# Attention, leaky-ReLU MLP and gated MLP on one core: results of the last layer turned in 32x32 blocks on VectorE and stored in runs of 64 features

## Chip, cores, metric

The kernel runs on one core of a Trainium2 chip. The metric is device time in microseconds (us), the median of several runs; smaller is better.

## What is computed

The reference, cut to its core (all in float32):

```python
# q, k, v: (8, 8, 576, 64); attention inside chunks of 64 positions
attn = softmax(q_c @ k_c.T / 8)              # per chunk
x = (attn @ v).transpose(0, 2, 1, 3).reshape(4608, 512)
h = x @ w_in                                  # 512 -> 2048
x = (max(h, 0) + alpha * min(h, 0)) @ w_out   # 2048 -> 512
g, val = x @ w_gate, x @ w_val                # 512 -> 1536 each
out = (silu(g) * val) @ w_out2                # 1536 -> 512, out is (4608, 512)
```

## The kernel before

**Layout.** Activations stand with features on the 128 partitions and tokens along the row. The 4608 tokens are nine blocks of 512 (`NB`); blocks 0 to 7 are the first 512 positions of each of the eight sequences, block 8 holds the last 64 of each. Every float32 product is three passes in `fp32r` (`mm3`, lines 522 to 524): an operand is split into a high part (a copy, ACT or VectorE) and a low part (a subtraction, VectorE), by `split`.

**Products of block pairs.** Two blocks are worked as a 2x2 block product with seven products in place of eight (numbers `p` 5, 1, 6, 2, 7, 3, 4 in `layer2`, `ORDER2`; 1 to 4 of operands `g`, 5 to 7 of sums). Each sums up in PSUM banks: X0, X1 for p 1, 6, 7, 4, one upon the other; W0, W1 for 5 and 3; Y0, Y1 for 2. So a bank X must be read between two of these products. Quarter `c` of the result (0 to 3: half `c // 2` of the 512 features, block `c % 2` of the pair), each in two tiles `m` of 128 features, is finished after p = 2 (c 0), 7 (c 3), 3 (c 1) and 4 (c 2).

**The last layer and its output.** `mlp_b` runs the gated MLP for the pairs (1, 2), (3, 4), (5, 8), (6, 7); its second layer hands each finished PSUM tile to `to_out` (line 762). There VectorE adds PSUM and a saved part into one of eight spare tiles (for c 2 a copy does), tokens along the row. Once a block has its four tiles, TensorE transposes them against `ident` into bank a0 or a1, four 128x128 pieces for each 128 tokens (line 781); a copy takes the bank to one of three tiles `c`, and `store_rows` (line 759) stores 128 tokens with 2 KB rows. Block 0 is computed the other way round, tokens on the partitions (`plain2(..., natural=True)`, line 661), and stored from `c` as it is. The weights of the last layer are split by `out2_quad` through `make` in the middle of the kernel, stored in `l_out2`, and read back by each pair.

**Order of the work.** All steps go into a `Program` with an engine, a guessed cost and their dependences. `order()` gives each step a due time from the main products that depend on it (a step on which no product depends has none and comes last) and lays the engines' streams in order of time. All DMAs are issued from SP, in that order; a DMA whose data are not there holds those behind it.

Of the kernel before, what the change touches and what calls it, by code (L numbers as in the profile page):

```python
# [13 lines left out]
ALU = mybir.AluOpType  # L14
# [3 lines left out]
P = 128  # L18
# [107 lines left out]
def act(n):  # L126
    return 0.17 + n * 0.84e-3


def dve2(n):  # L130
    return 0.15 + n * 1.05e-3
# [5 lines left out]
def dve1(n):  # L137
    return 0.1 + n * 0.53e-3
# [3 lines left out]
def attention_moe_moe2(ctx, tc, q, k, v, w_in, w_out, alpha, w_gate, w_val, w_out2, out):  # L142
# [24 lines left out]
    B, H, S, D = q.shape  # L167
# [3 lines left out]
    CH = 64  # L171
    KD = DM // P
    HP = H // 2
    NB = 512
    NCH = NB // CH
    NBLK = NT // NB
    JA = FF // (2 * P)
    JB = FF2 // (2 * P)
    scale = 1.0 / float(D) ** 0.5
    G = 256  # L180

    pr = Program()
    nv, na, ng, npe, nsp = nc.vector, nc.scalar, nc.gpsimd, nc.tensor, nc.sync
# [6 lines left out]
    def one(name, shape, dtype=F32):  # L190
        return sb.tile(shape, dtype, name=name, tag=name)

    KF = FF // P
    ident = one("ident", [P, P])
# [1 line left out]
    nalpha_sb = one("nalpha_sb", [P, KF])  # L196
    zero = one("zero", [P, KF])
    ops = Ring(sb, "op", 14, [P, 2, NB], F32R)
    gts = [[one(f"g{j}_{c}", [P, NB]) for c in range(4)] for j in range(JA)]
    xin = Ring(sb, "xin", 4, [P, NB], F32)  # L200
    sring = Ring(sb, "s", 6, [P, NB], F32)
    hring = Ring(sb, "h", 2, [P, NB], F32)
# [4 lines left out]
    cs = Ring(sb, "c", 3, [P, NB], F32)  # L207
# [8 lines left out]
    bank = {b: ps.tile([P, NB], F32, name=b, tag=b) for b in ("X0", "X1", "W0", "W1", "Y0", "Y1", "a0", "a1")}  # L216
# [4 lines left out]
    def item(engine, cost, fn, reads=(), writes=(), port=False, **kw):  # L221
        pr.add([(engine, cost, fn, port)], reads, writes, **kw)

    def dma(nbytes, fn, reads=(), writes=(), lat=2.2, **kw):
        item("SP", 0.06 + nbytes / 390e3, fn, reads, writes, lat=lat, **kw)


    def copy_(dst, src, n, reads, writes, psum=True, **kw):
        pr.add([("ACT", act(n), lambda: na.activation(out=dst, in_=src, func=AF.Copy), False),  # L229
                ("DVE", dvep(n) if psum else dve1(n), lambda: nv.tensor_copy(dst, src), not psum)],  # L230
               reads, writes, **kw)

    def add2(dst, a, b, op, n, reads, writes, psum=False, **kw):
        item("DVE", dve2(n), lambda: nv.tensor_tensor(out=dst, in0=a, in1=b, op=op), reads, writes, **kw)  # L234

    def split(hi, lo, src, n, rkeys, hkey, lkey, **kw):
        copy_(hi, src, n, rkeys, [hkey], psum=False, **kw)
        add2(lo, src, hi.bitcast(F32), ALU.subtract, n, [*rkeys, hkey], [lkey], **kw)
# [51 lines left out]
    lay_out2 = Layer("l_out2", [(j, p) for p in [*ORDER2, 21] for j in range(JB)])  # L290
# [4 lines left out]
    def rows(w, m):  # L295
        return w[m * P:(m + 1) * P, :]

    def convert(src, into=None, after=None):

        raw, rk = raws.next()  # L300
        rk = [rk, rk + (0,), rk + (1,)]
        c, ck = into or cs.next()
        dst = raw.rearrange("p a b -> p (a b)")
        if len(src.shape) == 3:
            dst = dst.rearrange("p (a f) -> p a f", a=src.shape[1])
        dma(NB * 8 * P, lambda: nsp.dma_start(out=dst, in_=src), [], rk, after=after)

        lw, lk = tring.next()  # L310
        lw, cu = lw.bitcast(U32), c.bitcast(U32)
        item("ACT", 0.66, lambda: na.activation(out=c, in_=raw[:, :, 1].bitcast(F32), func=AF.Abs, scale=2.0 ** -112),
             rk, [ck])
        item("DVE", 0.4, lambda: nv.tensor_scalar(out=lw, in0=raw[:, :, 0], scalar1=29, scalar2=None,
                                                   op0=ALU.logical_shift_right), rk, [lk], port=True)
        item("DVE", 0.69, lambda: nv.scalar_tensor_tensor(out=cu, in0=cu, scalar=3, in1=lw, op0=ALU.logical_shift_left,
                                                          op1=ALU.bitwise_or), [lk], [ck], port=True)
        item("DVE", 0.69, lambda: nv.scalar_tensor_tensor(out=cu, in0=raw[:, :, 1], scalar=0x80000000, in1=cu,
                                                         op0=ALU.bitwise_and, op1=ALU.bitwise_or),
             rk, [ck], port=True)  # L320
        return c, ck

    LO, HI = slice(0, G), slice(G, 2 * G)

    def sums(c0, k0, c1, k1, by_cols):

        if by_cols:
            a11, a12, a21, a22 = (c0[:, LO], k0), (c0[:, HI], k0), (c1[:, LO], k1), (c1[:, HI], k1)
        else:
            a11, a12, a21, a22 = (c0[:, LO], k0), (c1[:, LO], k1), (c0[:, HI], k0), (c1[:, HI], k1)  # L330
        ta, ka = tring.next()
        tb, kb = tring.next()
        s1, s2, s3, s4 = (ta[:, LO], ka), (ta[:, HI], ka), (tb[:, LO], kb), (tb[:, HI], kb)

        def comb(d, a, b, op):
            add2(d[0], a[0], b[0], op, G, [a[1], b[1]], [d[1]])

        comb(s1, a21, a22, ALU.add)
        comb(s2, s1, a11, ALU.subtract)
        comb(s3, a11, a21, ALU.subtract)  # L340
        comb(s4, a12, s2, ALU.subtract)
        return {1: a11, 2: a12, 3: s4, 4: a22, 5: s1, 6: s2, 7: s3, 21: a21}
# [10 lines left out]
                self.t, self.k = self.ring.next()  # L353
            return self.t[:, self.h], self.k + (self.h,)

    def make(layer, use, src, dst):

        t, key = dst
        split(t[:, 0], t[:, 1], src[0], G, [src[1]], key, key)
        layer.put(use, t, key)  # L360
        return t, key

# [358 lines left out]
    def silu(x, c, acc, b, s, n):  # L721
# [11 lines left out]
        else:  # L733
            add2(g, src, g, ALU.mult, n, rd, [gk, *wr], psum=s is None)


    spare = [(gts[j][c], ("g", j, c)) for j in range(JB, JB + 2) for c in range(4)]
    flip = [0]

    def row_runs(s0, n):  # L740

        runs, t = [], s0
        while t < s0 + n:
            i, r = divmod(t, NB)
            if i < B:
                m = min(s0 + n - t, NB - r)
                row = i * S + r
            else:
                c, r = divmod(r, CH)
                m = min(s0 + n - t, CH - r)  # L750
                row = c * S + NB + r
            runs.append((t - s0, m, row))
            t += m
        return runs

    def store_rows(e, ek, s0, w):
        def store():
            for a, k_, row in row_runs(s0, w):
                nsp.dma_start(out=out[row:row + k_, :], in_=e[a:a + k_])
        dma(w * NB * 4, store, [ek], [])  # L760

    def to_out(m, c, acc, b, s, n, pair, got):
        t, tk = spare[(2 * (c >= 2) + m) + 4 * (c % 2)]
        h = t[:, :n]
        if s is not None:
            add2(h, acc, s[0], ALU.add, n, [s[1]], [tk, b], psum=True)
        else:
            copy_(h, acc, n, [], [tk, b])
        col = c % 2
        got.setdefault(col, set()).add((c, m))  # L770
        if len(got[col]) < 4:
            return
        src = [spare[f + 4 * col] for f in range(KD)]
        for o0 in range(0, n, P):
            w = min(P, n - o0)
            bk = f"a{flip[0] % 2}"
            flip[0] += 1

            def tr(o0=o0, w=w, bk=bk):
                for f in range(KD):  # L780
                    npe.transpose(bank[bk][:w, f * P:(f + 1) * P], src[f][0][:, o0:o0 + w], ident)  # L781
            item("PE", 0.45, tr, [x[1] for x in src], [bk])
            e, ek = cs.next()
            copy_(e[:w], bank[bk][:w], NB, [], [ek, bk])

            store_rows(e, ek, pair[col] * NB + o0, w)

    def gkey(j, c):
        return gts[j][c], ("g", j, c)
# [32 lines left out]
    chalves = Halves(cring)  # L822
# [24 lines left out]
    def out2_quad(j, after):  # L847
        c = [z for m in (2 * j, 2 * j + 1) for z in convert(rows(w_out2, m), after=pr.mains[after])]
        bl = sums(*c, False)
        for p in (1, 21, 2, 4, 5, 6, 7, 3):  # L850
            make(lay_out2, (j, p), bl[p], chalves.next())

    with tc.manual_schedule():
        make_identity(nc, ident)
# [40 lines left out]
        def mlp_b(pair, weights, between=lambda: None):  # L895
            o = operands(x2d, "x2", pair, xin8)
            layer1(qb, NB, o, weights, act_b)
            between()
            layer2(JB, NB, lay_out2, partial(to_out, n=NB, pair=pair, got={}))
# [27 lines left out]
        x = load_x(x1d, "x1", 8)  # L927
# [4 lines left out]
        for j in range(4):  # L932
            out2_quad(j, m0 + 6 * j)
        m0 = len(pr.mains)
        mlp_a((4, 5), got_in)
        for j in range(4, JB):
            out2_quad(j, m0 + 20 * (j - 4))
# [4 lines left out]
        half = cring.t[0].bitcast(F32).rearrange("p h a g -> p h (a g)")  # L942
# [14 lines left out]
        plain2(JB, [(0, XW)], partial(stored, lay_out2, OUT, lambda j: j), natural=True)  # L957
        for a, b in enumerate(XW):
            e, ek = cs.next()
            copy_(e, bank[b], NB, [], [ek, b])  # L960
            store_rows(e, ek, a * P, P)

        assert sring.i % sring.n == 0
        mlp_b((1, 2), second_quads(lay_b, lambda x: [*keep[x][0], *keep[x][1]]))
# [8 lines left out]
        warm, t, seq = True, 0.0, pr.order()  # L973
        for s, _, engine, cost, fn, main in seq:
            if engine == "PE" and warm:
# [5 lines left out]
                t = s + cost  # L981
# [33 lines left out]
```

## Time and profile before

| | |
|---|---|
| runs | 1749.92, 1748.27, 1744.92 us; median 1748.27 |
| profiled execution | 1743.0 us, span of its instructions 1741.2 us |
| granted TensorE clock, mean | 0.989 of full |
| busy share of the span | TensorE 95%, its weight loads 78%, VectorE 70%, ScalarE 54% |
| DMA | 407.58 MB in 321588 packets; 73.3% of 16 engines' span |

A view's row gives what it says for one execution: busy time, how often, the mean of one, and what ended the idle time before. PE is TensorE, DVE is VectorE, ACT ScalarE; SPq rows are DMA issues of SP. A timeline row merges equal instructions that follow each other (x8) into start, length and form.

### The profile page before, as it was taken

The numbers are of one execution on the slowest core, as the hardware profiler recorded it, in microseconds if no ns is written. First come the engines' busy times: TensorE is split into PE (matmuls) and PEld (weight loads), VectorE is DVE, ScalarE is ACT, GpSimd is POOL, SyncE is SP. The second block draws the span as 40 slices with busy tenths as digits, with TensorE's granted clock in tenths as the row PEclk, the third lists the DMA queues.
The fourth block names the chain that finished last, engine by engine and source line by source line (L and its number), as shares of the span: only waits on it lengthen the run. The fifth ranks groups of instructions, "written<-read, shape, count | busy, mean of one in ns | idle before, by whom it ended". The sixth has DMA issues, their size and how long they took to land.

```text
span 1741.2 us, 26558 instructions
## 1 busy us (share of the span) xinstructions
PE 1661.1 (95%) x9388; PEld 1352.7 (78%) x9388; DVE 1215.6 (70%) x2156; ACT 935.7 (54%) x1649; POOL 1.0 (0%) x8
## 2 busy tenths in 40 slices
PE   6898998999889799999999999999999999999998
PEld 5777886778767577877888788778878888788886
DVE  5787886898666689777666954588769544864482
ACT  5677545774353677554444544464675533643362
POOL 0000000000000000000000000000000000000000
PEclk9999999999999899999999999999999999999999
DMA  8978878778999895888755577886765855555563
GB/s 197 261 246 242 283 260 266 239 215 237 248 264 308 315 354 190 274 269 291 267 196 188 191 217 235 221 248 217 235 211 190 285 195 193 189 199 193 193 209 129
DMA packets 321588, 407.58 MB, mean 234 GB/s; under 512 B 175280, under 2 KB 195760, under 8 KB 321456
## 3 DMA queue, kind: packets, MB, share of 16 engines
q1 hardware_dynamic: 319392, 405.89, 73.3%
q8 instruction: 74, 1.21, 0.3%
q14 instruction: 58, 0.48, 0.1%
q10 hardware_dynamic: 2064, 0.01, 0.1%
HBM read 307.24 MB, written 98.57 MB: 233 GB/s over the span
## 4 chain that ended last, share of the span: by engine, by line
PE 52%; DMA 2%; DVE 2%; ACT 1%; issue 0%; ACTq 0%; SPq 0%; DVEq 0%
PE X L522 9%; PE X L523 9%; PE X L524 9%; PE W L522 5%; PE W L524 5%; PE W L523 5%; PE Y L523 2%; PE Y L522 2%; PE Y L524 2%; DMA raw<-in_moe_w_gate_dram 1%; PE X L661 1%; PE W L661 1%; DMA raw<-in_moe_w_val_dram 1%; PE a L781 1%; PE a L465 0%
## 5 line engine op out<-in xcount | busy, mean ns | idle before, releaser
L522 PE MATMUL X<-op,w 128*128 128x512 f32 x1024 | 407.8, 398 | 19.1 <-DVE h L234 12.7
L523 PE MATMUL X<-op,w 128*128 128x512 f32 x1024 | 400.8, 391 | 0.0
L524 PE MATMUL X<-op,w 128*128 128x512 f32 x1024 | 400.6, 391 | 0.0
L229 ACT ACTIVATE op<-g 128x512 fp32r<-128x512 f32 x348 | 210.8, 629 | 146.1 <-PE X L523 43.9
L234 DVE TENSOR_TENSOR op<-g,op 128x512 fp32r<-128x512 f32 x348 | 227.3, 686 | 36.6 <-ACT op L229 31.2
L522 PEld LDWEIGHTS X<-op,w 128*128 128x128 f32 x1024 | 193.2, 189 | 70.6 <-DVE h L234 17.3
L522 PE MATMUL Y<-op,w 128*128 128x512 f32 x560 | 225.0, 402 | 4.1 <-ACT g L732 2.5
L524 PEld LDWEIGHTS X<-op,w 128*128 128x128 f32 x1024 | 193.4, 189 | 41.1
L522 PE MATMUL W<-op,w 128*128 128x512 f32 x544 | 214.0, 393 | 10.6 <-ACT h L229 10.6
L523 PEld LDWEIGHTS X<-op,w 128*128 128x128 f32 x1024 | 193.5, 189 | 37.8
L523 PE MATMUL Y<-op,w 128*128 128x512 f32 x560 | 220.1, 393 | 1.8 <-DVE w L234 1.8
L524 PE MATMUL Y<-op,w 128*128 128x512 f32 x560 | 219.9, 393 | 0.0
L524 PE MATMUL W<-op,w 128*128 128x512 f32 x544 | 212.4, 390 | 0.0
L523 PE MATMUL W<-op,w 128*128 128x512 f32 x544 | 212.2, 390 | 0.0
L229 ACT ACTIVATE s<-X 128x512 f32<-128x512 f32 x172 | 102.3, 596 | 107.5 <-PE X L524 106.2
L234 DVE TENSOR_TENSOR h<-Y,s 128x512 f32<-128x512 f32 x78 | 53.7, 689 | 137.7 <-PE Y L524 136.5
L522 PEld LDWEIGHTS Y<-op,w 128*128 128x128 f32 x560 | 106.5, 190 | 28.3 <-ACT g L732 2.9
L522 PEld LDWEIGHTS W<-op,w 128*128 128x128 f32 x544 | 102.4, 188 | 33.2 <-ACT h L229 11.4
L703 DVE SCALAR_TENSOR_TENSOR g<-h,nalpha_sb,g 128x512 f32<-128x512 f32 x143 | 106.7, 746 | 28.9 <-ACT h L695 28.6
L523 PEld LDWEIGHTS Y<-op,w 128*128 128x128 f32 x560 | 106.6, 190 | 23.8 <-DVE w L234 2.8
L524 PEld LDWEIGHTS Y<-op,w 128*128 128x128 f32 x560 | 106.1, 190 | 22.8
L524 PEld LDWEIGHTS W<-op,w 128*128 128x128 f32 x544 | 102.4, 188 | 21.6
(136 smaller groups left out, 2070.0 us busy)
## 6 DMA issues: line engine op xcount, KB each, us to landing
w<-l_out SPq DMA_DIRECT2D x168, 512.0 KB, 3.8
w<-l_b SPq DMA_DIRECT2D x126, 512.0 KB, 4.2
w<-l_in SPq DMA_DIRECT2D x56, 512.0 KB, 4.5
l_b<-w SPq DMA_DIRECT2D x84, 256.0 KB, 3.3
l_out<-cw SPq DMA_DIRECT2D x80, 256.0 KB, 5.0
l_in<-w SPq DMA_DIRECT2D x64, 256.0 KB, 4.0
raw<-in_moe_w_out_dram SPq DMA_DIRECT2D x28, 512.0 KB, 5.2
w<-l_in SPq DMA_DIRECT2D x56, 256.0 KB, 4.9
```

Of the source, the lines that this page charges most:

```text
L229: pr.add([("ACT", act(n), lambda: na.activation(out=dst, in_=src, func=AF.Copy), False), ("DVE", dvep(n) if psum else dve1(n), lambda: nv. ...
L234: item("DVE", dve2(n), lambda: nv.tensor_tensor(out=dst, in0=a, in1=b, op=op), reads, writes, **kw)
L522: npe.matmul(out=acc, lhsT=w[:, 0, wk], rhs=x[:, 0, :n], start=first, stop=False, skip_group_check=True)
L523: npe.matmul(out=acc, lhsT=w[:, 1, wk], rhs=x[:, 0, :n], start=False, stop=False, skip_group_check=True)
L524: npe.matmul(out=acc, lhsT=w[:, 0, wk], rhs=x[:, 1, :n], start=False, stop=stop, skip_group_check=True)
L661: npe.matmul(out=acc, lhsT=t[:, gp, a * P:(a + 1) * P], rhs=w[:, :, wp, :], start=first and i == 0, stop=stop and i == 2, skip_group_check ...
L703: nv.scalar_tensor_tensor(out=g, in0=h, scalar=nal, in1=g, op0=ALU.mult, op1=ALU.add)
L781: npe.transpose(bank[bk][:w, f * P:(f + 1) * P], src[f][0][:, o0:o0 + w], ident)
```

## The change

In `to_out` VectorE adds into one of the two tiles `h` (`hring`), then turns that tile in 32x32 blocks (`nv.transpose`) into a tile `turned`; for c 2 it turns straight from PSUM. A 32x32 turn leaves the tokens of a block of 32 on the partitions of their feature group, so a quarter is stored by four DMAs of 32 partitions, each with runs of 64 features (256 bytes); for block 8 by eight. For 64 consecutive features to meet, the columns of the last layer's weights are reordered when they are split (`make(..., turn=True)`), and for block 0 put back when its PSUM banks are copied, in halves of 256. The spare tiles of two `j` become four tiles `turned` of twice the width in the same place. TensorE's transposes, the copies from a0 and a1, and `store_rows` are gone.

```diff
-    gts = [[one(f"g{j}_{c}", [P, NB]) for c in range(4)] for j in range(JA)]
+    gts = [[one(f"g{j}_{c}", [P, NB]) for c in range(4)] for j in range(JB)]
+    turned = [one(f"turned{i}", [P, 2 * NB]) for i in range(2 * (JA - JB))]
+    gts += [[t[:, h * NB:(h + 1) * NB] for t in turned[2 * i:2 * i + 2] for h in range(2)] for i in range(JA - JB)]
...
+    def swapped(t, a, b):
+        return t.rearrange("p (a b i) -> p b a i", a=a, b=b)
...
-        split(t[:, 0], t[:, 1], src[0], G, [src[1]], key, key)
+        if turn:
+            split(swapped(t[:, 0], 2, 4), swapped(t[:, 1], 2, 4), src[0].rearrange("p (g m i) -> p g m i", g=4, m=2),
+                  G, [src[1]], key, key)
...
     def to_out(m, c, acc, b, s, n, pair, got):
-        t, tk = spare[(2 * (c >= 2) + m) + 4 * (c % 2)]
-        h = t[:, :n]
-        if s is not None:
-            add2(h, acc, s[0], ALU.add, n, [s[1]], [tk, b], psum=True)
-        else:
-            copy_(h, acc, n, [], [tk, b])
...
-            item("PE", 0.45, tr, [x[1] for x in src], [bk])
-            e, ek = cs.next()
-            copy_(e[:w], bank[bk][:w], NB, [], [ek, bk])
-            store_rows(e, ek, pair[col] * NB + o0, w)
+        col, half = c % 2, c // 2
+        k = 2 * col + half
+        e = turned[k].rearrange("p (t m i) -> p t m i", m=2, i=32)
+        if s is not None:
+            t, tk = hring.next()
+            h = t[:, :n]
+            add2(h, acc, s[0], ALU.add, n, [s[1]], [tk, b], psum=True)
+            rd, wr = [tk], []
+        else:
+            h, rd, wr = acc, [], [b]
+        item("DVE", 0.7, lambda: nv.transpose(out=e[:, :, m, :], in_=h.rearrange("p (t i) -> p t i", i=32)),
+             rd, [*ek, *wr])
...
+            for g in range(4):
+                gs, fs = slice(32 * g, 32 * g + 32), slice(2 * P * half + 64 * g, 2 * P * half + 64 * g + 64)
+                src = turned[k].rearrange("p (t f) -> p t f", f=64)[gs]
+                if i < B:
+                    nsp.dma_start(out=out[i * S:i * S + NB, fs].rearrange("(t p) f -> p t f", p=32), in_=src)
...
-            copy_(e, bank[b], NB, [], [ek, b])
-            store_rows(e, ek, a * P, P)
+            for h in (LO, HI):
+                copy_(e[:, h].rearrange("p (g m i) -> p g m i", g=4, m=2), swapped(bank[b][:, h], 2, 4), G, [],
+                      [ek, b])
```

**Where the order moves.** Line numbers below are those of each kernel's own file. TensorE's stream loses its 128 transposes and is otherwise the same, row for row. It ended, after the last product into X, with ten groups of four transposes; the last of these:

```order
L781 MATMUL a_163<-ident,g_0_105 128x128
L781 MATMUL a_163<-ident,g_1_106 128x128
L781 MATMUL a_163<-ident,g_2_107 128x128
L781 MATMUL a_163<-ident,g_3_108 128x128
L781 MATMUL a_164<-ident,g_0_105 128x128
L781 MATMUL a_164<-ident,g_1_106 128x128
L781 MATMUL a_164<-ident,g_2_107 128x128
L781 MATMUL a_164<-ident,g_3_108 128x128
```

Now the last product is TensorE's end, and VectorE's stream ends with the adds, the turns into `turned` (`h` are the two tiles of `hring`, X and W the banks of the product):

```order
L237 TENSOR_TENSOR h_119<-W_155,s_117 128x512
L237 TENSOR_TENSOR h_120<-W_156,s_118 128x512
L761 STREAM_TRANSPOSE turned_107<-h_119 128x16x32
L761 STREAM_TRANSPOSE turned_107<-h_120 128x16x32
L761 STREAM_TRANSPOSE turned_106<-X_153 128x16x32
L761 STREAM_TRANSPOSE turned_106<-X_154 128x16x32
```

Behind the last main product stand only two turns (from X) on VectorE, and SP's last four DMAs (of `turned_106`).

The other place is VectorE at the switch from the second layer of pair (1, 2) to the first layer of pair (3, 4), where it splits the next pair's operands (`op`, from `xin` and `raw`) between the last adds. Before:

```order
L234 TENSOR_TENSOR op_67<-raw_139,op_67 128x512
L234 TENSOR_TENSOR raw_139<-raw_139,xin_113 128x512
L234 TENSOR_TENSOR op_68<-raw_140,op_68 128x512
L234 TENSOR_TENSOR raw_140<-raw_140,xin_115 128x512
L234 TENSOR_TENSOR op_69<-xin_114,op_69 128x512
L234 TENSOR_TENSOR op_70<-xin_116,op_70 128x512
L234 TENSOR_TENSOR op_71<-raw_139,op_71 128x512
L234 TENSOR_TENSOR op_72<-raw_140,op_72 128x512
```

and now:

```order
L237 TENSOR_TENSOR op_67<-raw_135,op_67 128x512
L761 STREAM_TRANSPOSE turned_107<-h_119 128x16x32
L237 TENSOR_TENSOR op_68<-raw_136,op_68 128x512
L237 TENSOR_TENSOR raw_135<-raw_135,xin_109 128x512
L237 TENSOR_TENSOR op_69<-xin_110,op_69 128x512
L237 TENSOR_TENSOR raw_136<-raw_136,xin_111 128x512
L237 TENSOR_TENSOR op_70<-xin_112,op_70 128x512
L761 STREAM_TRANSPOSE turned_107<-h_120 128x16x32
L237 TENSOR_TENSOR op_71<-raw_135,op_71 128x512
L761 STREAM_TRANSPOSE turned_106<-X_153 128x16x32
L761 STREAM_TRANSPOSE turned_106<-X_154 128x16x32
L237 TENSOR_TENSOR op_72<-raw_136,op_72 128x512
```

Eight turns came in at this switch; the two that free X0 and X1 (ACT copies before) now stand behind the split of `op_71`.

On SP the quarter's four DMAs stand where the quarter is finished. Its stream ended with ten stores of 128 tokens; now it ends so (`w` are the weights read ahead):

```order
L262 DMA w_126<-l_out_167 128x1024
L773 DMA out_dram<-turned_105 32x16x64 x4
L262 DMA w_127<-l_out_167 128x1024
L773 DMA out_dram<-turned_108 32x16x64 x4
L773 DMA out_dram<-turned_107 32x16x64 x4
L773 DMA out_dram<-turned_106 32x16x64 x4
```

The first quarter's four DMAs moved ahead of the last weight load, and one quarter in place of ten row groups is left for the end.

## Rows read from the trace of the kernel before

**Rows 1.** Busy time by window: stretch, PE, PEld, DVE, ACT, POOL, clock, DMA share, GB/s.

```profile
500.00:600.00 100.00, 84.92 (x517) 67.50 (x516) 66.87 (x135) 45.60 (x92) 0.00 (x0) 0.91 0.93 296
1000.00:1100.00 100.00, 100.00 (x543) 82.42 (x543) 48.72 (x78) 43.71 (x71) 0.00 (x0) 1.00 0.76 226
1100.00:1200.00 100.00, 98.07 (x769) 78.20 (x768) 79.14 (x147) 55.84 (x89) 0.00 (x0) 1.00 0.84 233
1200.00:1300.00 100.00, 97.63 (x473) 80.27 (x472) 69.99 (x107) 67.24 (x116) 0.00 (x0) 1.00 0.66 223
1600.00:1700.00 100.00, 100.00 (x450) 82.79 (x449) 60.23 (x93) 47.20 (x82) 0.00 (x0) 1.00 0.58 200
```

**Rows 2.** Groups of instructions by line and form: busy us, mean ns.

```profile
L781 PE MATMUL a<-ident,g 128*128 128x128 f32 x128 | 17.8, 276 | 2.1 <-ACT c L229 2.0
L229 ACT ACTIVATE c<-a 128x512 f32<-128x512 f32 x32 | 18.3, 598 | 28.7 <-PE a L781 27.2 <-DMA out_dram<-c 0.8 <-PE W L523 0.2
L982 DVE STREAM_TRANSPOSE qT<-qk 128x512 f32<-128x512 f32 x20 | 14.1, 705 | 7.0 <-DMA qk<-in_q_dram 6.9
...
L234 DVE TENSOR_TENSOR g<-g,g 128x512 f32<-128x512 f32 x144 | 95.4, 685 | 0.9
L234 DVE TENSOR_TENSOR h<-X,s 128x512 f32<-128x512 f32 x78 | 53.6, 689 | 19.3 <-ACT g L732 8.7 <-PE X L524 5.3 <-DMA x2d<-h 2.3
L229 ACT ACTIVATE qT<-X 128x512 f32<-128x512 f32 x16 | 17.6, 1102 | 9.8 <-PE X L419 9.5 <-PE W L434 0.3
L229 ACT ACTIVATE cw<-c 128x256 fp32r<-128x256 f32 x24 | 9.7, 413 | 14.4 <-DMA l_out<-cw 13.5 <-DVE c L318 0.6 <-DVE h L234 0.3
```

**Rows 3.** Timeline of PE in the switch after pair (3, 4).

```profile
1281.67 0.39 PE L524 MATMUL X<-op,w 128*128 128x512 f32 x1
1281.90 1.04 PE L781 MATMUL a<-ident,g 128*128 128x128 f32 x8
1282.69 0.47 PE L522 MATMUL Y<-op,w 128*128 128x512 f32 x1
1283.01 0.39 PE L523 MATMUL Y<-op,w 128*128 128x512 f32 x1
1283.23 0.40 PE L524 MATMUL Y<-op,w 128*128 128x512 f32 x1
```

**Rows 4.** Timeline of PE, ACT and SP at the end.

```profile
1727.63 0.39 PE L524 MATMUL X<-op,w 128*128 128x512 f32 x1
...
1728.31 0.40 PE L524 MATMUL X<-op,w 128*128 128x512 f32 x1
1728.55 1.03 PE L781 MATMUL a<-ident,g 128*128 128x128 f32 x8
...
1737.53 0.60 ACT L229 ACTIVATE c<-a 128x512 f32<-128x512 f32 x1 [0.76 <-DMA out_dram<-c]
...
1729.81 8.67 SPq L759 DMA_DIRECT2D out_dram<-c  x10
```

**Rows 5.** Instructions on `out_dram` in the last 16 us.

```profile
L759 SPq DMA_DIRECT2D out_dram<-c x10: 332/332/338, 1729.8 to 1738.1; - x10
...
DMA to landing us min/median/max: 2.0/2.0/2.3
```

**Rows 6.** Timeline of DVE: two turns in a row.

```profile
1185.23 0.70 DVE L982 STREAM_TRANSPOSE qT<-qk 128x512 f32<-128x512 f32 x1
1185.86 0.67 DVE L982 STREAM_TRANSPOSE kT<-qk 128x512 f32<-128x512 f32 x1
```

**Rows 7.** Loads of `qk` (SP issue ns) and `v` (issue, landing), 1100 to 1200 us.

```profile
L397 SPq DMA_DIRECT2D qk<-in_q_dram x20: 332/487/1642, 1107.1 to 1177.5; - x20
...
L409 SPq DMA_DIRECT2D v<-in_v_dram x10: 601/618/1310, 1114.3 to 1173.8; - x10
DMA to landing us min/median/max: 3.0/5.3/7.7
```

**Rows 8.** Timelines at the first switch: ACT, DVE, PE.

```profile
1019.96 1.28 ACT L229 ACTIVATE g<-X 128x512 f32<-128x512 f32 x2 [0.23 <-PE X L524]
...
1019.77 0.69 DVE L234 TENSOR_TENSOR op<-raw,op 128x512 fp32r<-128x512 f32 x1 [0.66 <-ACT op L229]
...
1021.80 0.39 PE L522 MATMUL X<-op,w 128*128 128x512 f32 x1
```

**Rows 9.** Waits of PE, 1200 to 1300 and 1300 to 1400 us: us, times, longest.

```profile
PE X L522 <- DVE h L234: 1.7, 1, 1.7
...
PE X L522 <- DVE h L234: 1.5, 1, 1.5
```

**Rows 10.** The page's DMA queue (packets, MB, share) and a weight load's landing (us).

```profile
q1 hardware_dynamic: 319392, 405.89, 73.3%
...
w<-l_b SPq DMA_DIRECT2D x126, 512.0 KB, 4.2
```

More of the change, by code (lines that the diff above doesn't have):

```diff
@@ L354, in next, with make @@
             return self.t[:, self.h], self.k + (self.h,)
-    def make(layer, use, src, dst):
+    def swapped(t, a, b):
+        return t.rearrange("p (a b i) -> p b a i", a=a, b=b)
+    def make(layer, use, src, dst, turn=False):
         t, key = dst
-        split(t[:, 0], t[:, 1], src[0], G, [src[1]], key, key)
+        if turn:
+            split(swapped(t[:, 0], 2, 4), swapped(t[:, 1], 2, 4), src[0].rearrange("p (g m i) -> p g m i", g=4, m=2),
+                  G, [src[1]], key, key)
+        else:
+            split(t[:, 0], t[:, 1], src[0], G, [src[1]], key, key)
         layer.put(use, t, key)
@@ L734, in silu @@
             add2(g, src, g, ALU.mult, n, rd, [gk, *wr], psum=s is None)
[L737 to L747, printed above, removed]
-            else:
[L749 to L754, printed above, removed]
@@ L756, in store_rows, with to_out @@
-    def store_rows(e, ek, s0, w):
-        def store():
[L758 to L762, printed above, removed]
-        t, tk = spare[(2 * (c >= 2) + m) + 4 * (c % 2)]
-        h = t[:, :n]
-        if s is not None:
-            add2(h, acc, s[0], ALU.add, n, [s[1]], [tk, b], psum=True)
-        else:
-            copy_(h, acc, n, [], [tk, b])
[L769 to L781, printed above, removed]
-            item("PE", 0.45, tr, [x[1] for x in src], [bk])
-            e, ek = cs.next()
-            copy_(e[:w], bank[bk][:w], NB, [], [ek, bk])
-            store_rows(e, ek, pair[col] * NB + o0, w)
+    def to_out(m, c, acc, b, s, n, pair, got):
+        col, half = c % 2, c // 2
+        k = 2 * col + half
+        e = turned[k].rearrange("p (t m i) -> p t m i", m=2, i=32)
+        ek = [("g", JB + k // 2, 2 * (k % 2) + x) for x in range(2)]
+        if s is not None:
[3 more added lines that the diff above has]
+            rd, wr = [tk], []
+        else:
+            h, rd, wr = acc, [], [b]
+        item("DVE", 0.7, lambda: nv.transpose(out=e[:, :, m, :], in_=h.rearrange("p (t i) -> p t i", i=32)),
+             rd, [*ek, *wr])
+        got[c] = got.get(c, 0) + 1
+        if got[c] < 2:
+            return
+        i = pair[col]
+        def store():
+            for g in range(4):
[3 more added lines that the diff above has]
+                    nsp.dma_start(out=out[i * S:i * S + NB, fs].rearrange("(t p) f -> p t f", p=32), in_=src)
+                else:
+                    o3 = out.rearrange("(b s) f -> b s f", b=B)
+                    for a in range(2):
+                        nsp.dma_start(out=o3[:, NB + 32 * a:NB + 32 * a + 32, fs].rearrange("b p f -> p b f"),
+                                      in_=src[:, a::2, :])
+        dma(2 * P * NB * 4, store, ek, [])
@@ L850, in out2_quad @@
         for p in (1, 21, 2, 4, 5, 6, 7, 3):
-            make(lay_out2, (j, p), bl[p], chalves.next())
+            make(lay_out2, (j, p), bl[p], chalves.next(), turn=True)
     with tc.manual_schedule():
@@ L959, in attention_moe_moe2 @@
             e, ek = cs.next()
-            copy_(e, bank[b], NB, [], [ek, b])
-            store_rows(e, ek, a * P, P)
+            for h in (LO, HI):
+                copy_(e[:, h].rearrange("p (g m i) -> p g m i", g=4, m=2), swapped(bank[b][:, h], 2, 4), G, [],
+                      [ek, b])
+            dma(P * NB * 4, partial(lambda e, a: nsp.dma_start(out=out[a * P:(a + 1) * P, :], in_=e), e, a), [ek], [])
         assert sring.i % sring.n == 0
```

## Prediction

> **What bounds the kernel now.** I read the busy time by window first, because the change touches only the last 740 us and three earlier spots. From 1000 us on, where `to_out` works, TensorE is busy for 97.6 to 100% of each window shown, at a granted clock of 1.00 (2.4 GHz), while VectorE stands at 49 to 79%, ScalarE at 44 to 67% and the DMA engines at 58 to 84% [rows 1]. So in that stretch an instruction taken from TensorE is time taken from the kernel, as long as its neighbours keep up. Next the timeline, for what a transpose really holds TensorE; then the end, where TensorE no longer sets the pace: its last main product begins at 1728.31 us and the span ends at 1741.2, and in between a chain of transpose, copy and store through three tiles `c` runs step by step [rows 4]. Last I read VectorE and the waits at the switches between pairs, since VectorE takes over the work.
>
> **Removed, between products.** The mean of 276 ns for a transpose [rows 2] is its latency; the price is what it pushes back. Around a run of eight, the matmul ahead starts at 1281.67 and the second one behind at 1283.01, 1.34 us; two steps of the steady pace (1283.01 to 1283.23, with rounding 0.225) would be 0.45. Eight transposes cost 0.89 us [rows 3]. Of 128, 40 stand behind the last product; the other 88 are eleven such runs: 11 x 0.89 = **-9.8 us**. With them go 32 copies of 598 ns on ScalarE [rows 2]. These cost nothing today as ScalarE is not the bound, except perhaps around 1290 to 1302 us, where TensorE waits 1.7 and 1.5 us for VectorE [rows 9] just after ScalarE has worked through eight of them. I take 0 for that, with -3.2 as the end on the good side.
>
> **The end.** Before: 1728.71 (1728.31 + 0.40, the last product's end) to 1741.2, 12.5 us. After: the turn of X0 can begin when its last matmul is done, at 1727.63 + 0.39, say 1728.1. A turn of 128x512 takes 0.70 us [rows 2, 6], two in a row start 0.63 apart [rows 6]. Here they read PSUM, which no turn before did; adds from PSUM take 689 ns against 685 from SBUF [rows 2], so I keep 0.70: both are done at 1729.45. Then SP issues four DMAs. A plain store takes it 0.33 us [rows 5]; the patterned loads of `qk`, also 32 partitions each, take 0.49, those of `v` 0.62 [rows 7]. At 0.49, nearest in shape, the last issue starts at 1731.0. Each DMA has 32 x 16 = 512 runs of 256 bytes, the count and size of a `v` load; that lands in 3.0 us at best and 7.7 at worst [rows 7], where a store of whole rows with little else queued lands in 2.0 [rows 5]. I take 3.5 us, near the best, since little else is moving, but all four run at once: 1734.5. Before, 1.1 us lay between the last landing (1738.1 + 2.0) and the end; so 1735.6, **-5.6 us**. The ends: landing in 2.0 gives 1734.1 (-7.1), in 7.7 gives 1739.8 (-1.4). The quarter of p = 3 is stored some 6 us earlier and is out of the way.
>
> The Trainium skill (DMA: Bandwidth & Descriptors, Specifications) asks for 512 bytes or more per transfer for line rate and says that a DMA engine does a read-modify-write below that; it gives no price. It speaks against this change, which goes from 2 KB to 256-byte runs. By it the sum is nearer -10.0 than -14.2, or worse (first and third rival); no store in the trace before is that short, so no row shows it.
>
> **Added on VectorE.** 32 turns of 0.70 us; the adds were there. Eight come at each of the three switches, 8 x 0.63 = 5.0 us each. They are covered by VectorE's idle half. What can lose the cover is one place: banks X0 and X1 used to be emptied by ScalarE from 1019.96 us, and TensorE wanted X0 again at 1021.80 [rows 8]. Now the turn of X0 stands behind the split of `op_71`, whose counterpart ended at 1019.77 + 0.69 = 1020.46 [rows 8]; X0 is free at 1021.16, 0.64 us in time, and X1 is not wanted before the next group of products. Six other turns ahead make VectorE a little late, so I put 0.3 us for each switch, **+1.0 us**; the ends are 0 and 1.5 each (the longer waits that TensorE had for VectorE were 1.7 and 1.5 [rows 9]), 4.5 in all. On SP a quarter's four issues (2.0 us) replace two plain ones (0.7 us [rows 5]); behind them wait weight loads, which run ahead by six of seven tiles `w`, each good for twelve matmuls: 6 x 12 x 0.227 = 16.3 us, less a landing of 4.2 [rows 10], 12.1 us of lead. I cost that at 0.
>
> **Weights and block 0.** The 48 splits with reordered columns handle as many elements in runs of 32; I keep 413 ns [rows 2]. The far row is a copy that writes every fourth element, 1102 ns for 512 [rows 2], 1.85 times a contiguous one of 598. At that price ScalarE and VectorE would have some 17 us more each, in a stretch where TensorE is idle for 15.1 of 100 us, at a mean clock of 0.91 [rows 1]; a fifth more of that idle time, 3.0 us, is my high end, an estimate. The copies that free block 0's banks become two of about 0.41 us in place of one of 0.60: the first bank is 0.2 us later, **+0.2 us**, ends 0 and 0.9 (all four).
>
> **Sum:** -9.8 - 5.6 + 1.0 + 0.2 = **-14.2 us**, from the profiled execution's 1743.0 us to 1728.8. That execution lies 5.3 us under the median of the runs, 1748.27, and under the fastest of them, so for a median I forecast 1748.27 - 14.2 = **1734 us**.
>
> **Rivals.** *First, short runs land slowly.* The last quarter lands after 7.7 us: -9.8 - 1.4 + 1.2 = -10.0, **1738 us**. For it: that landing was seen, for loads of this shape, with the DMA engines at 84% in that window [rows 1]. Against it: the end has nothing else in flight. *Second, VectorE becomes the bound at the switches.* If each of the 24 turns there delays TensorE in full, 24 x 0.63 = 15.1 us in place of 1.0, -14.2 + 14.1 gives **1748 us**, no change. For it: the window with the second switch has VectorE at 70% and ScalarE at 67% [rows 1]. Against it: the order puts work without a due time last, and 70% leaves 30 us in 100 for 5. *Third, the other side: the 256-byte packets hold up the weight loads.* A quarter is 2048 packets, 128 for each engine. The mean packet of the queue takes 0.733 x 16 x 1741.2 us / 319392 = 64 ns [rows 10]. If a short store costs that, a quarter takes 8.2 us of all engines, and one is finished every 36 x 0.227 = 8.2 us, while the weights take 58% of the engines [rows 1]: 4.8 us left over per quarter, 19.2 per switch, less the lead of 12.1, so TensorE stands for 7.1 us at each of three switches, 21.3; at the end the last two quarters queue, landing at about 1741.4, so +1.3 there. -9.8 + 1.2 + 21.3 + 1.3 = +14.0, **1762 us**. It decides from a price of 50 ns (4 x (128 x 50 ns - 3.4) = 12). Against it: the best `v` load moved its 32 packets per engine in 1.0 us beyond the 2.0 of a nearly empty queue [rows 5, 7], about 31 ns.
>
> **Chances.** A change of 0.3%, 5.2 us, is about what a measurement of this kernel can tell from none. My forecast has 0.67, the first rival 0.15, the second 0.10 (half of its price or more), the third 0.05, anything else 0.03. Forecast and first rival are faster, and about half of the second: **faster 0.87**. The rest of the second and some of the unknown make **same 0.07**; the third and a little make **slower 0.06**. All good ends together give -9.8 - 7.1 - 3.2 = -20.1, 1728, and two more for the scatter of runs (1744.92 to 1749.92): 1726. On the other side 1743 takes in the first rival, with the bounds of the switches. The 80% range is **1726 to 1743 us**.
>
> **What would show it.** Right: `to_out`'s transposes gone and no new gaps, TensorE at 99% or more from 1000 us on, last product about 10 us earlier, 6 to 8 us from its end to the span's; turns of about 0.70 us. Wrong: a new wait of TensorE for VectorE's turn of X at three switches (second rival); turns from PSUM or splits by 32 that are longer than their rows; last landings of 5 us and more (first); weight loads that land after 10 us and TensorE waiting for `w` (third). A gain under 8 us would mean that the products between do not close up.

## The result and the profile after

| | before | after |
|---|---|---|
| median of 6 runs | 1746.60 us | 1729.54 us (1724.21 to 1736.13) |
| profiled execution | 1743.0, span 1741.2 us | 1724.21, span 1722.4 us |

The ratio is 0.9917, with a 95% interval of 0.9895 to 0.9938: 14.5 us faster, between 10.8 and 18.3 (the two medians alone stand 17.1 us apart). Two later sets of runs of the same pair gave 0.9927 (0.9910 to 0.9944) and 0.9938 (0.9922 to 0.9954). So the change is worth under 1%, and each interval leaves out 1. The forecast was 1734 us in a range of 1726 to 1743.

Three of the windows of [rows 1], and then all waits of TensorE from 1000 us on, of the changed kernel (waited for: us in total, times, longest):

```profile
1000.00:1100.00 100.00, 99.31 (x552) 81.18 (x551) 55.66 (x92) 39.49 (x63) 0.00 (x0) 1.00 0.81 231
1200.00:1300.00 100.00, 96.01 (x414) 78.37 (x413) 76.37 (x117) 66.89 (x116) 0.00 (x0) 0.98 0.69 222
1600.00:1700.00 100.00, 99.17 (x436) 81.39 (x435) 63.62 (x100) 46.26 (x78) 0.00 (x0) 1.00 0.59 193
```

```profile
PE X L533 <- DVE h L237: 3.9, 4, 1.5
PE X L533 <- ACT s L232: 3.1, 5, 0.7
PE X L533 <- issue: 1.8, 1, 1.8
PE a L476 <- ACT pT L232: 0.7, 1, 0.7
```

The same list of the kernel before:

```profile
PE X L522 <- DVE h L234: 4.8, 4, 1.7
PE a L781 <- ACT c L229: 2.0, 4, 0.8
PE X L522 <- ACT s L229: 1.8, 3, 0.7
PE a L465 <- ACT pT L229: 0.7, 1, 0.7
```

Read together, these lines already say where the forecast's size is off. These windows of TensorE did not rise, they fell a little, and the one with the second switch lost clock (0.98). The waits for ScalarE's copies `s` went from three to five, and a wait of 1.8 us appeared that the profile gives to no engine ("issue"). Below, the *second switch* is the one at about 1205 to 1245 us, after pair (3, 4).

Instructions on `turned` from 1000 us on, of the changed kernel (times of one in ns, min/median/max), and the end:

```profile
L773 SPq DMA_DIRECT2D out_dram<-turned x52: 316/509/2092, 1003.0 to 1718.6; - x52
L761 DVE STREAM_TRANSPOSE turned<-h x21: 668/702/706, 1002.1 to 1709.4; 128x512 f32<-128x512 f32 x21
...
L761 DVE STREAM_TRANSPOSE turned<-X x8: 674/709/718, 1013.2 to 1716.4; 128x512 f32<-128x512 f32 x8
...
DMA to landing us min/median/max: 1.8/3.7/6.9
```

```profile
1715.69 1.40 DVE L761 STREAM_TRANSPOSE turned<-X 128x512 f32<-128x512 f32 x2 [5.58 <-PE X L535]
...
1715.95 0.39 PE L535 MATMUL X<-op,w 128*128 128x512 f32 x1
1717.12 2.18 SPq L773 DMA_DIRECT2D out_dram<-turned  x4
```

A turn costs 0.70 us from SBUF and 0.71 from PSUM, and the last product ends 6.1 us before the span does, where it was 12.5 [rows 4].

### The profile page after: what moved, and what is told of

Read it like the earlier page. It is cut to its first block, busy times and chain, and to the rows that moved or that the text cites. A ratio compares the mean times of both kernels' runs of the same rounds, so it can differ in the third digit from the quotient of the medians.

```text
span 1722.4 us, 26328 instructions
## 1 busy us (share of the span) xinstructions
PE 1644.0 (95%) x9260; PEld 1336.3 (78%) x9260; DVE 1232.2 (72%) x2188; ACT 915.0 (53%) x1614; POOL 1.0 (0%) x8
## 3 DMA queue, kind: packets, MB, share of 16 engines
q1 hardware_dynamic: 348640, 405.89, 75.1%
## 4 chain that ended last, share of the span: by engine, by line
PE 52%; DMA 2%; DVE 2%; ACT 1%; issue 0%; DVEq 0%; SPq 0%; ACTq 0%
PE X L533 9%; PE X L534 9%; PE X L535 9%; PE W L533 5%; PE W L535 5%; PE W L534 5%; PE Y L534 2%; PE Y L535 2%; PE Y L533 2%; PE X L672 1%; DMA raw<-in_moe_w_gate_dram 1%; PE W L672 1%; DMA raw<-in_moe_w_val_dram 1%; PE a L476 1%; DVE h L237 0%
## 5 line engine op out<-in xcount | busy, mean ns | idle before, releaser
L232 ACT ACTIVATE op<-g 128x512 fp32r<-128x512 f32 x300 | 182.3, 629 | 125.4 <-PE X L534 44.4
L237 DVE TENSOR_TENSOR op<-g,op 128x512 fp32r<-128x512 f32 x300 | 195.6, 685 | 27.5 <-ACT op L232 22.9
L237 DVE TENSOR_TENSOR h<-Y,s 128x512 f32<-128x512 f32 x86 | 58.9, 689 | 142.7 <-PE Y L535 141.7
L533 PEld LDWEIGHTS W<-op,w 128*128 128x128 f32 x544 | 102.4, 188 | 31.7 <-ACT h L232 9.7
L535 PEld LDWEIGHTS W<-op,w 128*128 128x128 f32 x544 | 102.4, 188 | 21.4
L534 PEld LDWEIGHTS W<-op,w 128*128 128x128 f32 x544 | 102.5, 188 | 21.0
```

The source lines that it names most:

```text
L533: npe.matmul(out=acc, lhsT=w[:, 0, wk], rhs=x[:, 0, :n], start=first, stop=False, skip_group_check=True)
L534: npe.matmul(out=acc, lhsT=w[:, 1, wk], rhs=x[:, 0, :n], start=False, stop=False, skip_group_check=True)
L535: npe.matmul(out=acc, lhsT=w[:, 0, wk], rhs=x[:, 1, :n], start=False, stop=stop, skip_group_check=True)
```

## Where the time went, by aligned products

The 6624 main products stand in the same order in every kernel of this study, so I set the k-th one of a kernel beside the k-th of the kernel before and take the difference of their starts. Each column is the difference gained (-) or lost (+) in one stretch of the products, in us: up to product 3500 (978 us), to 4000 (1098, with 32 transposes), to 4500 (1234, the second switch), to 4900 (1332, 32 transposes), to the last (24 transposes); "net" is the sum without the first column, "end" the time from the last product's end to the span's.

```
profiled execution    up to   978-    1098-   1234-   1332-    net    end
                      978     1098    1234    1332    last
before                 0       0       0       0       0       0      12.5
before_again          +1.8     0       0       0       0       0      12.5
after                 -7.2    -2.8    +3.7    -5.6    -0.5    -5.2     6.1
after_again           +8.9    -2.8    +3.7    -5.5    -0.6    -5.2     6.1
after_third           +1.3    -2.8    +3.7    -5.5    -0.5    -5.1     6.1
quarter_transposes    +3.6    +0.7     0       0      -0.6    +0.1    12.0
turns_left_out        -2.3    -2.7    +2.1    -5.5    -0.6    -6.7     5.5
turns_twice           +2.0    -1.4    +5.0    -5.5    +0.7    -1.2     7.5
long_runs             -1.5    -2.8    +2.1    -5.6    -0.6    -6.8     5.1
two_queues            +5.6    -2.8    +2.1    -5.5    -0.6    -6.8     7.0
earlier_copies        -2.0    -2.8    +0.1    -5.5    -0.6    -8.9     6.1
earlier_again         +4.9    -2.8    +0.1    -5.5    -0.6    -8.8     6.1
own_ring              +5.5    -2.5     0      -5.6    -0.7    -8.7     6.0
```

From 978 us on an execution repeats within about 0.1 us wherever the clock stays up; ahead of that the same kernel lies anywhere from 7 us early to 9 us late, so an effect of the change of a few us there would not show. The last two columns give the change -5.2 - 6.4 = -11.6 us. What the first set of runs shows above that, 2.9 us, is inside its interval, and the two later sets, -12.7 and -10.8, lie on either side.

## The experiments

**The two kernels once more.** No edit.

> The kernel before, once more. In the two profiles at hand the changed kernel's main products stand 7.2 us earlier already at about 830 us, where nothing of the change has been touched yet. Theory (chance of one execution): this second profile of the same kernel differs from the first by several us, up or down, in the same stretch up to 830 us; the time is within 0.3% of the kernel before. Rival (the early lead belongs to the change, for instance through the places of tiles in memory): the two profiles of before agree within 1 us up to 830 us.

> The changed kernel, once more, for the ratio and for a second profile. Theory: 0.990 to 0.994 of the kernel before; of its gain 5 to 6 us stand between the products (11 runs of eight transposes at 0.89 us = 9.8, given back in part at the second switch between pairs, where TensorE waited 1.8 us for a subtraction behind three turns and then ran at a granted clock of 0.81 to 0.84), and 6 to 6.5 us behind the last product. The second switch shows a wait of 1.5 us or more and the low clock again. Rival: the wait at the second switch was chance; this profile has none there, and the products end about 4 us earlier against 830 us than in the first profile.

> The changed kernel once more, beside the two kernels below on the same chip. Theory: between 1000 us and the last product it gains 5.2 us on the kernel before, as in both profiles so far, and 6.4 behind it; up to 1000 us it may lie several us either way. The wait of 1.8 us at the second switch is there. The time is 0.991 to 0.994 of before. Rival (the loss at the second switch comes and goes with the run): -7 to -9 us between the products in this profile.

Measured: before_again 0.9985 (0.9973 to 0.9998) of before. A kernel set against itself can thus miss 1 by 0.15%, 2.6 us, with an interval that leaves it out; differences of that size are read from the aligned products and not from the ratios. Its products stand 1.8 us later up to 978 us and exactly on those of before from there on. after_again (0.9927) stands 8.9 us late where the first profile of the same kernel stood 7.2 early. So the early lead belongs to an execution, not to the change. The loss at the second switch is in all three profiles of the changed kernel, 3.7 us each time.

**What a run of transposes costs TensorE.** The kernel before with one transpose of each four:

```diff
-                for f in range(KD):
+                for f in range(1):
                     npe.transpose(bank[bk][:w, f * P:(f + 1) * P], src[f][0][:, o0:o0 + w], ident)
```

> The kernel before with one of each four transposes; three quarters of the output of blocks 1 to 8 are left out of the banks. All adds, copies and stores stay. Theory (a run of eight costs TensorE 0.89 us because each takes 0.11 us of its stream): eleven runs of two cost 11 x 0.22 = 2.4 in place of 9.8 us, so 7.3 us less between the products, and 0 to 3 us less behind the last one: 1736 to 1740 against a before of 1746.6. Rival (most of the price is the switch to and from transposes, or lies under waits anyway): under 3 us between the products.

Measured: 0.9998 (0.9982 to 1.0014), 0.1 us lost between the products. The rival's number held (under 3 us), its reason only in part: a run does shrink from 0.89 to 0.23 us where nothing else is late, but three lay under waits, and the rest was lost to new ones. PE of this kernel, and then PE and one copy of ScalarE of the kernel before, at the first switch:

```profile
1026.49 0.39 PE L524 MATMUL X<-op,w 128*128 128x512 f32 x1
1026.73 0.38 PE L781 MATMUL a<-ident,g 128*128 128x128 f32 x2
1027.57 0.51 PE L522 MATMUL X<-op,w 128*128 128x512 f32 x1 [0.47 <-ACT s L229]
```

```profile
1022.93 0.39 PE L524 MATMUL X<-op,w 128*128 128x512 f32 x1
1023.17 1.03 PE L781 MATMUL a<-ident,g 128*128 128x128 f32 x8
1024.02 0.50 PE L522 MATMUL X<-op,w 128*128 128x512 f32 x1
...
1023.36 0.60 ACT L229 ACTIVATE s<-X 128x512 f32<-128x512 f32 x1 [0.76 <-PE X L524]
```

From product to product it is 1.08 and 1.09 us: two transposes and a wait, or eight and none. X is not free before ScalarE has copied it to `s`, and in the kernel before that copy ends at 1023.96, just ahead of the product. In the changed kernel, without any transpose, the same place, its like at the third switch and the place of the eight transposes near 1668 us of before each have a bare wait:

```profile
1016.79 0.50 PE L533 MATMUL X<-op,w 128*128 128x512 f32 x1 [0.69 <-ACT s L232]
...
1545.95 0.50 PE L533 MATMUL X<-op,w 128*128 128x512 f32 x1 [0.69 <-ACT s L232]
...
1657.23 0.50 PE L533 MATMUL X<-op,w 128*128 128x512 f32 x1 [0.82 <-DVE h L237]
```

So three runs of eight lay on time in which TensorE would have stood anyway. What the shorter runs did save here was lost to new waits: at 1085 us 2.3 us for ScalarE's `c` (the copies of the transposes, [rows 2], still stood there), and near 1296 us 2.4 us for VectorE's `h`, behind which the clock fell (0.70 in 1295 to 1300).

**What makes the wait at the second switch: the turns?** The changed kernel with a copy of 32 columns in place of each turn, in the same order:

```diff
-        item("DVE", 0.7, lambda: nv.transpose(out=e[:, :, m, :], in_=h.rearrange("p (t i) -> p t i", i=32)),
+        item("DVE", 0.7, lambda: nv.tensor_copy(e[:, 0, m, :], h[:, :32]),
```

> The changed kernel with each turn replaced by a copy of 32 columns on VectorE: the tiles stored hold no results of blocks 1 to 8. Order, stores and adds are the same. Theory (at the second switch the three turns on VectorE make the subtraction for the next operand late): the wait of 1.8 us there and the low clock after it are gone, 3 to 4 us between the products, and the end is 1.2 us shorter (two turns in a row): 4 to 5 us under the changed kernel. Rival (the stall there comes from the stores, from loads or from ScalarE): the stall stays, and only the 1.2 us at the end go.

Measured: 0.9923 (0.9900 to 0.9945). My theory fell: the wait is there, 1.82 us, to the hundredth what it was with the turns. Only the low clock behind it is missing, which is 1.6 of the 3.7 us, and which two runs with every turn in place miss as well (long_runs, two_queues). At the end 0.6 us went, not 1.2, since the first turn runs beside the last product.

A wait of the same length with and without the turns points at something that hangs on TensorE's own progress. The timelines show how. ACT and then DVE of the changed kernel:

```profile
1217.16 0.63 ACT L705 ACTIVATE g<-h 128x512 f32<-128x512 f32 x1 [1.99 <-DVE h L237]
1217.83 0.63 ACT L706 ACTIVATE h<-h 128x512 f32<-128x512 f32 x1
1220.01 0.60 ACT L232 ACTIVATE s<-W 128x512 f32<-128x512 f32 x1 [1.55 <-PE W L535]
1220.51 1.14 ACT L232 ACTIVATE op<-raw 128x512 fp32r<-128x512 f32 x2
```

```profile
1217.67 1.25 DVE L237 TENSOR_TENSOR raw<-raw,xin 128x512 f32<-128x512 f32 x2
1218.84 0.75 DVE L714 SCALAR_TENSOR_TENSOR g<-h,nalpha_sb,g 128x512 f32<-128x512 f32 x1
1221.16 1.29 DVE L237 TENSOR_TENSOR op<-raw,op 128x512 fp32r<-128x512 f32 x2 [1.57 <-ACT op L232]
1222.37 0.68 DVE L237 TENSOR_TENSOR h<-X,s 128x512 f32<-128x512 f32 x1
```

ScalarE's two copies into `op` have their data at 1218.92 but stand behind `s<-W`, which waits for a product of TensorE that ends at 1219.98. VectorE's subtractions wait for the copies, and behind them stands `h<-X`, which alone frees X. TensorE goes on at 1223.16. In the order of before both copies stood ahead of that copy of W. If the order is the cause, another order takes the wait away with all turns in place.

**The order alone.** The price that the planner reckons for a turn, and nothing else; a few rows of the order change, all between some 1180 us and the second switch:

```diff
-        item("DVE", 0.7, lambda: nv.transpose(
+        item("DVE", 0.6, lambda: nv.transpose(
```

> The changed kernel with the planner's price of a turn at 0.6 in place of 0.7; the order then differs in a few rows, all around the second switch: ScalarE's copies into op_4 and op_5 stand ahead of the copy of W1 and no longer behind it. Theory (the wait of 1.8 us at the second switch is made by that order: the copies wait for W1, the subtractions behind them on VectorE for the copies, and the add that frees X0 for both): the copies start 2.05 us earlier (1218.46 in place of 1220.51 by the first profile of the changed kernel), X0 is free in time or up to 0.3 us late, the clock stays at 1.00, and between 1200 and 1245 us TensorE gains 1.5 to 3.4 us on the changed kernel: -5.2 between 1000 us and the last product becomes -6.7 to -8.6. Rival (the wait has another cause, for it lasted 1.82 us with and without turns): it stays, and -5.2 too.

> The changed kernel with the planner's price of a turn at 0.6, once more. Theory: by the rows its gain on the changed kernel is 3.6 us (the wait of 1.8 us at the second switch and the low clock behind it): 0.9890 to 0.9915 of the kernel before, 2 to 4 us under the changed kernel in the same set of runs. Rival (what it saves is lost again in other executions): the two stand within 1 us of each other.

Measured: 0.9913 (0.9894 to 0.9932) and, in the set with after_third, 0.9918 (0.9898 to 0.9938, just outside the 0.9915 expected) against 0.9938. The rows show what the ratios can't: in both profiles the stretch went from +3.7 to +0.1, and the net to -8.9 and -8.8, a little beyond the -8.6 expected. All waits of TensorE from 1205 to 1245 us, and ACT, of earlier_copies:

```profile
PE X L533 <- ACT s L232: 0.7, 1, 0.7
```

```profile
1222.60 0.63 ACT L706 ACTIVATE h<-h 128x512 f32<-128x512 f32 x1
1223.14 1.23 ACT L232 ACTIVATE op<-raw 128x512 fp32r<-128x512 f32 x2
1225.23 0.60 ACT L232 ACTIVATE s<-W 128x512 f32<-128x512 f32 x1 [0.86 <-PE W L535]
```

**The same order by another edit.** The adds go into four idle tiles of the attention in place of `hring`; the price stays 0.7:

```diff
+    oring = Ring.of([(qkt[0], "qT"), (qkt[1], "kT"), (pp, "pp"), (pT, "pT")])
...
-            t, tk = hring.next()
+            t, tk = oring.next()
```

> The changed kernel with the adds of the last layer going into four tiles of the attention's that are not in use at a switch (qT, kT, pp, pT) in place of the two tiles h that the layer before the last uses as well. The planner then also puts the copies into op_4 and op_5 ahead of that of W1, at an unchanged price of 0.7. Theory (the order on ScalarE makes the wait at the second switch): no wait over 0.5 us there, -8.5 to -9.2 us between 1000 us and the last product. Rival (it was something else in the price of 0.6): the wait of 1.8 us is there.

Measured: 0.9909 (0.9886 to 0.9933), -8.7 us between the products, no wait at the second switch but the 0.7 us that before has too. The second edit moves many other rows on VectorE, the first only a few; in both the copies stand ahead of that of W, and in both the wait is gone. With the chain in the timelines that settles its cause. Both versions beat the three profiles of the changed kernel, by 3.5 to 3.7 us in the rows, and by about 2 us those executions with its order in which the clock stayed up (+2.1 at the second switch); in this set the medians were 1743.86 (before), 1734.94 (after), 1731.21 (price of 0.6) and 1730.58 us (own tiles).

**Does VectorE have room?** Every turn twice:

```diff
-        item("DVE", 0.7, lambda: nv.transpose(out=e[:, :, m, :], in_=h.rearrange("p (t i) -> p t i", i=32)),
+        def turn():
+            for _ in range(2):
+                nv.transpose(out=e[:, :, m, :], in_=h.rearrange("p (t i) -> p t i", i=32))
+        item("DVE", 0.7, turn,
```

> The changed kernel with every turn made twice in a row into the same tile, 32 more of 0.70 us on VectorE. Theory (VectorE has room at the switches; what a turn costs there is at most what it adds to a chain that TensorE waits for): +0.3 to +1.5 us between 1000 us and the last product, all of it at the second switch, and +1.3 to +1.4 us behind the last product. Rival (VectorE is the bound at the switches): each of 24 turns costs 0.63 us, +15 us between the products.

Measured: 0.9957 (0.9937 to 0.9977); 4.0 us more between the products and 1.4 at the end. I had expected 0.3 to 1.5, all at the second switch; it was 1.3 us at each of the three. The rival's 15 us is out. Waits of TensorE at the first switch, 1005 to 1075 us:

```profile
PE X L533 <- DVE turned L763: 1.1, 1, 1.1
PE X L533 <- ACT s L232: 0.7, 1, 0.7
```

The first of the two is new (the changed kernel has only the second): of the eight turns at a switch it is one from PSUM, that of X, which TensorE can wait for. Made once, it is done in time.

**Run length.** Each quarter stored as runs of 4 KB (2 KB in block 8), in other places of the output:

```diff
-                        src = turned[k].rearrange("p (t f) -> p t f", f=64)[gs]
+                        src = turned[k][gs]
...
-                    nsp.dma_start(out=out[i * S:i * S + NB, fs].rearrange("(t p) f -> p t f", p=32), in_=src)
+                    nsp.dma_start(out=out[r0:r0 + 64, :].rearrange("(p a) f -> p (a f)", a=2), in_=src)
```

> The changed kernel with each quarter of 32 partitions stored as runs of 4 KB (2 KB for block 8) to rows of its own: the same bytes and the same number of DMAs, the output of blocks 1 to 8 stands in other places. Theory (a store of 512 runs of 256 bytes lands about 1 us later than one of long runs, and costs nothing else): last landings 2.0 to 2.2 us in place of 3.0, so 0.8 to 1.0 us off the end, nothing between the products. Rival A (run length is of no account): landings of 2.8 to 3.0 and no change. Rival B (short runs hold up the weight loads): TensorE gains 2 us or more between the products.

Measured: 0.9913 (0.9880 to 0.9946); the end is 5.1 us, 1.0 less. Landings of the last stores (after from 1700 us, then long_runs from 1715 us):

```profile
DMA to landing us min/median/max: 2.2/2.8/3.0
```

```profile
DMA to landing us min/median/max: 1.9/2.1/2.3
```

Between the products it gained nothing but the low clock, which this execution did not have (+2.1, as in two_queues with the 256-byte runs). So 256-byte runs cost about 1 us once, at the end. The rule of the Trainium skill (DMA: Bandwidth & Descriptors, Specifications), 512 bytes or more for line rate, points the right way; here its price is that 1 us.

**Two queues at the end.** Two of the last four stores issued by ScalarE.

```diff
+        if pair == (6, 7) and c == 2:
+            dma(P * NB * 4, lambda: store((0, 2), nsp), ek, [])
+            item("ACT", 0.4, lambda: store((1, 3), na), ek, [], lat=2.2)
```

> The changed kernel with the last quarter's four stores issued two by SP and two by ScalarE. Theory (behind the last turn the four issues of some 0.5 us each stand in a row on SP, and the last landing counts from the fourth): the fourth issue is 0.8 to 1.0 us earlier and the end of 6.1 us becomes 5.1 to 5.4. Rival (issuing on ScalarE costs as much as it saves, or the four landings share one path): 5.9 us or more.

Measured: 0.9938 (0.9919 to 0.9958), an end of 7.0 us, 0.9 longer:

```profile
L773 SPq DMA_DIRECT2D out_dram<-turned x2: 316/316/316, 1728.2 to 1731.4; - x2
L773 ACTq DMA_DIRECT2D out_dram<-turned x2: 380/444/507, 1728.2 to 1728.7; - x2
```

ScalarE issued its two in a row, but SP's second store came 3.2 us after its first. The waits of SP's queue from 1725 us on name a landing of another store:

```profile
SPq L773 <- DMA out_dram<-turned: 2.8, 1, 2.8
```

In the trace SP's second store and ScalarE's first count their landings on the same counter; ScalarE's first landed at 1731.39 us, and SP's second began at 1731.40. So one waited for the other, and the experiment says nothing about two queues as such; that stays open.

## Why the prediction was right, and where its sum was off

The direction, the range and the winning case held; the sum of -14.2 us was 2.6 too large against the rows' -11.6, and its parts were further off than the total. That the total came so near is in part luck: the transposes gave 2.8 us less than forecast and the switches cost 2.7 more, while the waits of [rows 9] gave 2.0 and the end 0.8 that were not in the sum. One sign named for being right was not met: TensorE was to be busy for 99% or more from 1000 us on, and stood at 96.0% in the window with the second switch.

- **"Eight transposes cost 0.89 us ... eleven such runs: -9.8 us."** This step failed in part. The 88 transposes stand in nine runs of eight and four of four, which alone changes little, for the price of one is nearly the same. It is right where TensorE has nothing else to wait for: 24 transposes gave 2.8 us in 978 to 1098 (2.67 by the price). But three runs of eight lay on waits for X, which took their place: 0 in place of 2.7. The run near 1687 us gave 0.6 in place of 0.9, as the product behind it now starts late for X. The gap around each of them was in the trace before, and so was the step that frees X and ends just when the product goes on (ScalarE's copy `s<-X` at two of them, VectorE's `h<-X` near 1668 us); I had measured only the cheapest run [rows 3] and multiplied.
- **"I take 0 for that, with -3.2 as the end on the good side"** for the waits of [rows 9]. It came out at -2.0: 32 transposes give 3.6 by their price, and the stretch gained 5.6. Of the waits of 1.7 and 1.5 us one is left. In quarter_transposes, where ScalarE's copies stay, the wait of 1.7 us grew to 2.4; so the transposes did not make it. The copies' places on ScalarE are the likely cause, but the planner's order differs there too (one step that VectorE made of `g` near 1290 us is ScalarE's now), and no run holds the two apart.
- **"I put 0.3 us for each switch, +1.0 us."** Mis-sized and for another reason. Two switches cost nothing. The second cost 3.7 us: 1.82 us of wait, the restart, and the low clock in four of the seven executions with that order. I had read VectorE's load; what decided was a place in ScalarE's order, which I had set beside that of before only at the first switch and the end.
- **"The end ... -5.6 us"** was -6.4. The turns were done 0.75 us after the last product (0.74 forecast), the last issue began at 2.24 (2.29), it landed in 2.9 (3.5 taken, 2.0 and 7.7 as ends), and 0.9 us lay behind it in place of 1.1.
- **Weights and block 0, +0.2:** hardly to be seen. The splits by 32 take 412 ns against 413 [rows 2], and across block 0 the difference of the products goes from -7.22 to -7.16, a loss of 0.06 us that every profile with the change repeats.

The first rival (a landing of 7.7 us) did not occur at the end. The second (24 turns of 0.63) is out by turns_twice. The third (short packets that hold up weight loads) is out: DMA time on the queue rose from 73.3% [rows 10] to 75.1%, a load from `l_b` lands in 4.3 us in place of 4.2, and no wait of TensorE from 1000 us on names a weight tile:

```profile
q1 hardware_dynamic: 348640, 405.89, 75.1%
...
w<-l_b SPq DMA_DIRECT2D x126, 512.0 KB, 4.3
```

## What to carry to other kernels

Price a removed instruction at each of its places: ask what the next product waits for besides, and subtract what was only covered. When a planner orders the streams, a new step also moves old ones; look at the order around every wait of the bound engine, for a changed guess of 0.1 us was worth 2.0 to 3.6 us here. Where runs of a kernel differ by 10 us in a stretch that a change does not touch, align the instructions of two profiles and read the difference by stretch.

## What the runs showed of the hardware that was not expected

The clock after one and the same wait is not fixed. In the 1.82 us at the second switch TensorE stood still in after, after_again, after_third, turns_left_out, long_runs and two_queues alike. Behind it the first three had some eight matmuls at steps of 0.43 us in place of 0.23, which is the lower level, 1.2 GHz; the granted clock of after was 0.84 in the 5 us of the wait and 0.81 in the next 5, and 0.50 from 1224 to 1226 us:

```profile
1220.00:1225.00 5.00, 3.18 (x11) 2.28 (x11) 3.79 (x6) 3.95 (x7) 0.00 (x0) 0.84 0.81 207
1225.00:1230.00 5.00, 5.00 (x19) 3.99 (x19) 2.47 (x5) 2.41 (x6) 0.00 (x0) 0.81 1.06 274
...
1224.00:1225.00 1.00, 1.00 (x4) 0.81 (x3) 0.99 (x2) 0.95 (x2) 0.00 (x0) 0.50 0.96 292
1225.00:1226.00 1.00, 1.00 (x3) 0.74 (x3) 0.41 (x2) 0.69 (x2) 0.00 (x0) 0.50 1.27 284
```

In the last three the clock stayed at 1.00. The fall costs 1.6 us (+3.7 against +2.1 at the second switch); what decides whether it comes was not tried.
